# Gated mix of linear attention and a GEGLU block on one core: the handover from the first stage to the units, with a pool for the first stage's last results and a new order

## The chip, the cores and the metric

The kernel runs on one core of one Trainium2 chip. The metric is the device time in microseconds of one execution; lower is better. Three runs of the kernel before took 2373.40, 2373.74 and 2373.41 us, median 2373.41.

## The reference

All arrays are float32. `x` is 2048 tokens of 1024; 32 heads of 32; the inner width of the second block is 3584.

```
x = A_x
g = sigmoid((x * gate_w).sum(-1, keepdims=True))
q, k, v = split of x @ wqkv into heads
pq, pk  = q @ w_phi, k @ w_phi                       (per head)
phi(t)  = concat(softmax(t), softmax(-t))
kv = sum over s of phi(pk)^T v ;  z = sum over s of phi(pk)
a = ((phi(pq) @ kv) / (phi(pq) . z + 1e-6)) @ wo
b = (gelu(x @ w_gate) * (x @ w_up)) @ w_down
out = g * a + (1 - g) * b
```

## The kernel before, in words

Every float32 operand of a matmul is split into a high and a low half (ScalarE copies the high half, `high` L421 or `split` L43; VectorE subtracts for the low half, `low` L424 or L44), and three matmuls of the four products are made (`PASSES`). So a product of 128 x 1024 by 1024 x 512 is 24 matmuls of 128x512, and one over four blocks of 128 is 12.

The kernel has three parts.

*The first stage* (to L412; pools kw and kp, PSUM pools pd and pg) makes the keys and values for all tokens, their features, and sums kv and z over the tokens. Its last pieces are the tail of this study: `finish_kv` (L242) adds up kv in `kv_t` with `kv_l` and transposes it into `kv_c` (L254), which GpSimd's queue writes to the scratch tensor `kz` (L257); `finish_z` (L264) copies z into `zb` (L272), written to `kz` at L412. Both `kv_c` and `zb` are tiles of the pool kp. VectorE also makes `g_at` there, sixteen copies of 32x16 out of the gates `g_a` (L405 to L407); it is read only much later, by `attention` (L892). The first stage already makes some products of the second block: `first_g`, `first_u` (both halves of column block 0, on banks of pd), whose weights are in `first_w`.

*The handover* (L631 to L688, on all four engines written in the order in which the code stands, for VectorE, ScalarE, TensorE and SyncE). `gs` and `us` (L111, by `project`) are the gate and up products of column block 1, 2 x 24 matmuls each, on the four banks of pg. `gate_up` (L647) turns a gate product and an up product into a block of hidden values: gelu on ScalarE (L650), the product on VectorE (L651), and `spill` on GpSimd's queue into the scratch tensor `lm` (L139). The result `h` is a tile with three buffers (`hidden`, L476). At the same time `x_sums` (L485, VectorE, L488 to L491) makes four sums and differences of blocks of x out of a `raw` tile, for each of four `kc`; `highs` and `lows` make the halves of the four operands `xs` (tiles s1 to s4) from them. The raw tiles of kc 0 to 2 lie in the pool mid, the fourth in fp. `fp`, like `xa`, takes the place of kp, and a tile waits for everything that still uses the place where it lies. `start(weights(0, ...))` and `drain` let the generator that makes the first unit's weights take its steps (`wgu` for x, `tyz` for y and z, `v`).

*The units* (L764 on): 62 units of seven products of 12 matmuls, a Strassen-like scheme that makes four blocks out of seven products, on PSUM pools `pl` (a twice, p, c) and `pe` (c11, b, misc twice). `pe` lies where pg lay. The order of VectorE, ScalarE and SyncE in them comes from a planner: each generator yields (earliest slot, latest slot, VectorE's cost, ScalarE's cost), and `run_slot` lets those step for which there is room in a slot of 2.65. `background` runs the attention and the second half's sums in the slots' spare time, beginning with a first attention job in slot 13. `begin(t)` (L700) is one matmul that opens a bank for accumulation; before, all three `seeds` (c11, b, c) are begun right after the first product of the first unit (L783 to L785). After the units comes a last part (L1138 and so on) that multiplies by `wo` and `w_down`.

Of the kernel before, what the change touches and what calls it, by code (L numbers as in the profile page):

```python
# [8 lines left out]
F32 = mybir.dt.float32  # L9
# [7 lines left out]
P = 128  # L17
# [14 lines left out]
def tile_gated_mix(ctx: ExitStack, tc: tile.TileContext, x, xT, wkT, wqT, wv, w_phi, wo,  # L32
# [104 lines left out]
    def spill(h, dst, j, m):  # L137

        nc.gpsimd.dma_start(dst[m // 4][j, m % 2, :, m // 2 % 2, :], h)  # L139
# [9 lines left out]

    PE, DVE, ACT, SP = (getattr(mybir.EngineType, n) for n in ("PE", "DVE", "Activation", "SP"))  # L150
    with tc.tile_pool(name="kw", bufs=1) as kw, tc.tile_pool(name="kp", bufs=1) as kp, \
            tc.manual_schedule(engines={PE, DVE}):
        ones = kp.tile([P, P], F32, name="ones")
        nc.vector.memset(ones, 1.0)
        ones_r = kp.tile([P, P], F32R, name="ones_r")
# [86 lines left out]
        def finish_kv(hh, pkv):  # L242

            t = kp.tile([P, 4, 2, 2, 64], F32, tag="e", name="kv_t", bufs=2)
            for n, p in enumerate(pkv):
                nc.scalar.activation(t[:, n], p[:, :, 0], AF.Copy)
                nc.vector.tensor_tensor(t[:, n], p[:, :, 1], t[:, n], OP.add)
            low_rows = kp.tile([P, 4, 2, 2, 64], F32, tag="e", name="kv_l", bufs=2)
            nc.scalar.activation(low_rows[:64], t[64:], AF.Copy)
            nc.vector.tensor_tensor(t[:64], t[:64], low_rows[:64], OP.add)  # L250
            kv_c = kp.tile([P, 4, 2, 2, 32], F32, name="kv_c")
            for h in range(2):
                q = slice(32 * h, 32 * h + 32)
                nc.vector.transpose(kv_c[q].rearrange("p a b c d -> p (a b c) d"),  # L254
                                    t[q].rearrange("p a b c d -> p (a b c) d")[:, :, q])
            for s in range(2):
                nc.gpsimd.dma_start(kz[0][64 * s:64 * s + 64, 4 * hh:4 * hh + 4], kv_c[:64, :, :, s])  # L257
# [144 lines left out]
        nc.scalar.activation(g_a, logit, AF.Sigmoid)  # L402
        nc.vector.tensor_scalar(g_b, g_a, -1.0, 1.0, OP.mult, OP.add)
        nc.vector.tensor_scalar(g_n, g_a, 1.0, -1.0, OP.mult, OP.add)
        for h in range(4):  # L405
            for q in range(4):
                nc.vector.tensor_copy(g_at[32 * h:32 * h + 32, :, q], g_a[32 * q:32 * q + 32, :])  # L407
# [15 lines left out]
    def low(dst, src, dst_h):  # L423
        nc.vector.tensor_tensor(dst, src, dst_h.bitcast(F32), OP.subtract)  # L424
# [13 lines left out]
    with tc.tile_pool(name="xa", bufs=1) as xa, tc.tile_pool(name="fp", bufs=1) as fp, \  # L438
            tc.manual_schedule(engines={PE, DVE, ACT, SP}):
        xs = [(xa if k < 2 else fp).tile([P, 2, KC // 2, BLK], F32R, name=f"s{k + 1}") for k in range(4)]  # L440

# [27 lines left out]

        def hold(*parts):
            held.append(True)
            return len(held) - 1, stage(*parts, pool=fp if len(held) % 4 == 0 else None)

        def hidden():  # L476
            return fp.tile([P, BLK], F32, tag="h", name="h", bufs=3)


        def x_load(half, kc, r1, r2):  # L480
# [25 lines left out]
        def second_half(t, staging):  # L506
# [6 lines left out]

            while not free[0]:
                yield now[0] + 1, NEVER, 0.0
            raw = fp.tile([P, 2, 2 * BLK], F32, tag="pts", name="raw", bufs=1)
            staging = [*staging, raw[:, 0], raw[:, 1]]

            def load(n):
# [112 lines left out]
        raws.append(fp.tile([P, 2, 2 * BLK], F32, tag="pts", name="raw", bufs=1))  # L632
        for kc, r in enumerate(raws):
            if kc == 3:
                staged_up = stage((0, 1024, w_up[1]))
# [8 lines left out]
            for k, kc in which:  # L644
                low(xs[k][:, 1, kc, :], sums[kc][k], xs[k][:, 0, kc, :])

        def gate_up(g, u, m, js=range(2)):  # L647
            for j in js:
                h = hidden()
                nc.scalar.activation(h, g[j], AF.Gelu_apprx_tanh)  # L650
                nc.vector.tensor_tensor(h, u[j], h, OP.mult)  # L651
                spill(h, left_mlp[0], j, m)

        gs = [project(second_w, j) for j in range(2)]

# [18 lines left out]
        drain(-5)  # L674
        gate_up(gs, us, 1, [0])
        drain(-4)
        highs((2, 1), (3, 1))
        lows((2, 1), (3, 1))
        drain(-3)
        gate_up(gs, us, 1, [1])  # L680
        drain(-1)
        highs((2, 2), (3, 2), (2, 3), (3, 3))

        def late_lows():

            for at, which in ((1, [(2, 2), (3, 2)]), (4, [(2, 3)]), (6, [(3, 3)])):
                yield at, at, 0.7 * len(which)
                lows(*which)  # L688

# [74 lines left out]
        def unit(n, half, kind, m, before):  # L764
# [6 lines left out]
            for k in range(7):  # L771
                moved = True
                if k == 0 and before:
                    nc.scalar.activation(c, b, AF.Copy)
                elif k == 1:
                    nc.scalar.activation(c11, a, AF.Copy)
# [24 lines left out]
                kind_of[0] = kind, k  # L801
                run_slot(7 * n + k, 0.7 if fill else 0.0, 0.6 * moved + 1.2 * fill)
# [37 lines left out]
        def attention(jobs, between):  # L840
# [4 lines left out]
            while more:  # L845
# [54 lines left out]
                pts = fp.tile([P, 2, 2, BLK], F32R, tag="pts", name="pts", bufs=1)  # L900
# [279 lines left out]
```

## Time and profile before

| what | value |
| --- | --- |
| runs | 2373.40, 2373.74, 2373.41 us |
| profiled execution | 2372.92 us, of which the span is 2371.2 |
| TensorE busy in the span | 2358.3 us (99%) |
| VectorE busy | 1798.8 us (76%) |
| ScalarE busy | 1059.2 us (45%) |
| granted TensorE clock | 1.00 |
| the handover in the span | about 431 to 475 us |
| the units | about 461 to 1682 us |

In the views, PE is TensorE, PEld its weight load, DVE VectorE, ACT ScalarE, POOL GpSimd, SP SyncE; a q behind a name means the engine's queue, which issues and waits. A row of the timeline has the start, the length of the group of equal instructions in microseconds, the engine, the line, the operation, the tile written and those read, the shape and the count; in brackets stands how long the engine was idle before it and what released it. A view of waits has the waiting instruction, what it waited for, and then the total, the number of times and the longest.

### The profile page before, as it was taken

How to read it: one execution, taken by the hardware profiler on the slowest of the kernel's cores; microseconds unless marked ns; L12 is line 12 of the kernel's file. 1: busy time of each engine (PE TensorE's matmuls, PEld its weight loads, DVE VectorE, ACT ScalarE, POOL GpSimd, SP SyncE). 2: the span in 40 equal slices, each digit the busy share in tenths (PEclk: the TensorE clock that was granted, in tenths of full speed). 3: DMA queues.
4: the chain of work that ended last, by engine and by line, in shares of the span. 5: the costliest groups of instructions: out<-in, count | busy, mean ns of one | idle time of the engine just before them, and what ended most of it. 6: DMA issues, size and time to landing. Idle time of an engine off the chain costs nothing.

```text
span 2371.2 us, 28231 instructions
## 1 busy us (share of the span) xinstructions
PE 2358.3 (99%) x10625; PEld 1955.7 (82%) x10625; DVE 1798.8 (76%) x2321; ACT 1059.2 (45%) x1384; POOL 159.2 (7%) x297
## 2 busy tenths in 40 slices
PE   9999999999999999999999999999999999999999
PEld 8888888788888788888888888888888888888887
DVE  7887878878888787777778877888674868867873
ACT  4324332446455545455565656565533222323221
POOL 0000000011111011110000000000000000000000
PEclk9999999999999999999999999999999999999999
DMA  5112233554444366673444434434684767977874
GB/s 179 46 45 89 83 125 107 171 184 160 171 165 172 135 211 208 209 278 131 132 150 149 143 134 148 143 134 148 245 293 168 270 226 247 340 267 274 290 264 137
DMA packets 152617, 425.10 MB, mean 179 GB/s; under 512 B 21408, under 2 KB 21408, under 8 KB 152480
## 3 DMA queue, kind: packets, MB, share of 16 engines
q1 hardware_dynamic: 123840, 329.30, 41.3%
q0 software_dynamic: 27600, 93.87, 10.2%
q8 instruction: 83, 1.36, 0.2%
q14 instruction: 54, 0.44, 0.1%
q10 hardware_dynamic: 1040, 0.13, 0.0%
HBM read 328.34 MB, written 94.90 MB: 178 GB/s over the span
## 4 chain that ended last, share of the span: by engine, by line
PE 77%; DVE 2%; ACT 1%; issue 0%; DVEq 0%
PE po L1138 29%; PE a L743 20%; PE c L743 13%; PE b L743 7%; PE p L743 7%; PE misc L920 1%; ACT x L874 0%; DVE tyz L424 0%; DVE st L879 0%; ACT L874 0%; DVE x L882 0%; DVE x L869 0%; DVE h L720 0%; ACT h L924 0%; DVE wgu L424 0%
## 5 line engine op out<-in xcount | busy, mean ns | idle before, releaser
L206 PE MATMUL pd<-wkv,x 128*128 128x512 f32 x1536 | 359.8, 391 | 0.0
L206 PEld LDWEIGHTS pd<-wkv,x 128*128 128x128 f32 x1536 | 284.7, 188 | 57.2 <-DVE x L44 0.3
L1138 PE MATMUL po<-tw,wgu 128*128 128x512 f32 x1344 | 309.8, 389 | 0.0
L1138 PEld LDWEIGHTS po<-tw,wgu 128*128 128x128 f32 x1344 | 252.3, 188 | 52.4
L421 ACT ACTIVATE wgu<-stage 128x1024 fp32r<-128x1024 f32 x147 | 155.3, 1056 | 239.6 <-DVE stage L1028 161.4
L424 DVE TENSOR_TENSOR wgu<-stage,wgu 128x1024 fp32r<-128x1024 f32 x147 | 179.1, 1218 | 71.5 <-ACT wgu L421 70.6
L743 PE MATMUL a<-s,tyz 128*128 128x512 f32 x744 | 180.5, 390 | 2.1 <-DVE tyz L424 1.4
L743 PE MATMUL b<-s,tyz 128*128 128x512 f32 x744 | 179.0, 389 | 1.2 <-ACT b L778 1.2
L743 PE MATMUL a<-x,wgu 128*128 128x512 f32 x744 | 179.4, 390 | 0.7 <-DVE wgu L424 0.7
L743 PE MATMUL p<-s,tyz 128*128 128x512 f32 x744 | 179.1, 389 | 0.0
L743 PE MATMUL c<-x,tyz 128*128 128x512 f32 x744 | 178.8, 389 | 0.0
L743 PE MATMUL c<-x,wgu 128*128 128x512 f32 x744 | 178.7, 389 | 0.0
L743 PE MATMUL a<-s,v 128*128 128x512 f32 x744 | 178.7, 389 | 0.0
L421 ACT ACTIVATE tyz<-stage 128x1024 fp32r<-128x1024 f32 x126 | 132.7, 1053 | 91.0 <-DVE stage L569 37.7
L424 DVE TENSOR_TENSOR tyz<-stage,tyz 128x1024 fp32r<-128x1024 f32 x126 | 153.2, 1216 | 21.5 <-ACT tyz L421 21.2
L743 PEld LDWEIGHTS a<-s,tyz 128*128 128x128 f32 x744 | 139.1, 188 | 33.7 <-DVE tyz L424 3.6
L743 PEld LDWEIGHTS b<-s,tyz 128*128 128x128 f32 x744 | 139.5, 188 | 31.0 <-ACT b L778 2.0
L743 PEld LDWEIGHTS a<-x,wgu 128*128 128x128 f32 x744 | 139.0, 188 | 31.0 <-DVE wgu L424 1.1
L743 PEld LDWEIGHTS p<-s,tyz 128*128 128x128 f32 x744 | 139.4, 188 | 29.7 <-ACT x L756 0.6
L743 PEld LDWEIGHTS c<-x,tyz 128*128 128x128 f32 x744 | 139.6, 188 | 29.1
L743 PEld LDWEIGHTS a<-s,v 128*128 128x128 f32 x744 | 139.6, 188 | 29.0
L743 PEld LDWEIGHTS c<-x,wgu 128*128 128x128 f32 x744 | 139.6, 188 | 29.0
(189 smaller groups left out, 3530.7 us busy)
## 6 DMA issues: line engine op xcount, KB each, us to landing
stage<-lm SPq DMA_DIRECT2D x98, 512.0 KB, 4.7
sr<-in_w_down SPq DMA_DIRECT2D x84, 512.0 KB, 4.7
sl<-lm SPq DMA_DIRECT2D x70, 512.0 KB, 4.7
lm<-h POOLq DMA_DIRECT2D x112, 256.0 KB, 2.7
stage<-in_w_gate SPq DMA_DIRECT2D x43, 512.0 KB, 4.2
stage<-in_w_up SPq DMA_DIRECT2D x43, 512.0 KB, 4.1
stage<-la SPq DMA_DIRECT2D x28, 512.0 KB, 5.1
tg<-stage POOLq DMA_DIRECT2D x26, 512.0 KB, 3.0
```

Of the source, the lines that this page charges most:

```text
L206: nc.tensor.matmul(ps[m], xb[b, kc // 4][:, a, kc % 4, t * P:(t + 1) * P], w[:, e, m * 512:(m + 1) * 512], start=kc == 0 and i == 0, stop= ...
L421: nc.scalar.activation(dst, src, AF.Copy)
L424: nc.vector.tensor_tensor(dst, src, dst_h.bitcast(F32), OP.subtract)
L743: nc.tensor.matmul(dst, w[:, h, 4 * part + kc, :], xq[:, e, kc, :], start=first and kc == 0 and i == 0, stop=kc == 3 and i == 2, skip_grou ...
L920: nc.tensor.matmul(po[p], kbs[:, p].rearrange("p a b -> p (a b)"), pts[:, q, p, :], start=q == 0, stop=q == 1)
L1138: nc.tensor.matmul(ps[c], lefts[s][:, a, m, c * P:(c + 1) * P], made[k][:, e, m], start=d == 0 and m == 0 and n == 0, stop=d == n_duo - 1 ...
```

## The change

Five edits in the handover:

1. `zb` and `kv_c` go into a pool `kl` of their own. Of the second pool set, a part goes into a new pool `fa`, opened before fp: s3 and s4, the fourth raw tile and `pts` (which share a tag), the fourth staging tile, and h. fp keeps the rest (v, kz, kb, kbs, mm, st).
2. The 16 copies of `g_at` leave the first stage and are made by `background` in the units, four at a time from slot 9 on, planned with 0.8 each. `background` takes no other step before.
3. `gate_up` is cut into `gelu` and `multiply`, and the handover is written in another order: the up weights' low half right behind their high half, the gelus ahead of the high halves that stood in front of them, and the low halves of s2 of kc 2 and 3 later, in `late_lows`.
4. The drains of the first unit's weights stand at other places of this order.
5. `begin` is called for one seed each in the products k = 0, 3 and 6 of the first unit.

```
-            tc.manual_schedule(engines={PE, DVE}):
+            tc.tile_pool(name="kl", bufs=1) as kl, tc.manual_schedule(engines={PE, DVE}):
-        zb = kp.tile([P, NG, 2, 32], F32, name="zb")
+        zb = kl.tile([P, NG, 2, 32], F32, name="zb")
-            kv_c = kp.tile([P, 4, 2, 2, 32], F32, name="kv_c")
+            kv_c = kl.tile([P, 4, 2, 2, 32], F32, name="kv_c")
...
-        for h in range(4):
-            for q in range(4):
-                nc.vector.tensor_copy(g_at[32 * h:32 * h + 32, :, q], g_a[32 * q:32 * q + 32, :])
...
-        xs = [(xa if k < 2 else fp).tile(...) for k in range(4)]
+        xs = [(xa if k < 2 else fa).tile(...) for k in range(4)]
...
-        def gate_up(g, u, m, js=range(2)):
-            for j in js:
-                h = hidden()
-                nc.scalar.activation(h, g[j], AF.Gelu_apprx_tanh)
-                nc.vector.tensor_tensor(h, u[j], h, OP.mult)
-                spill(h, left_mlp[0], j, m)
+        def gelu(g):
+            h = hidden()
+            nc.scalar.activation(h, g, AF.Gelu_apprx_tanh)
+            return h
+
+        def multiply(h, u, j, m):
+            nc.vector.tensor_tensor(h, u, h, OP.mult)
+            spill(h, left_mlp[0], j, m)
...
         high(flat(up_w)[0], staged_up)
-        gate_up(first_g, first_u, 0)
         low(flat(up_w)[1], staged_up, flat(up_w)[0])
+        us = [project(up_w, j) for j in range(2)]
+        highs((2, 0), (3, 0))
+        for j in range(2):
+            multiply(gelu(first_g[j]), first_u[j], j, 0)
         lows((1, 0))
-        highs((2, 0), (3, 0))
         add(3)
-        us = [project(up_w, j) for j in range(2)]
+        hs = [gelu(gs[0])]
         start(weights(0, *units[0]))
         now[0] = -20
-        lows((2, 0), (3, 0), (1, 1), (1, 2), (1, 3))
-        drain(-5)
-        gate_up(gs, us, 1, [0])
+        lows((2, 0), (3, 0))
         drain(-4)
+        hs.append(gelu(gs[1]))
+        drain(-3)
         highs((2, 1), (3, 1))
+        lows((1, 1))
+        multiply(hs[0], us[0], 0, 1)
+        drain(-1)
         lows((2, 1), (3, 1))
-        drain(-3)
-        gate_up(gs, us, 1, [1])
-        drain(-1)
+        multiply(hs[1], us[1], 1, 1)
...
-                    if n == 0:
-                        for t in seeds:
-                            begin(t)
...
+                if n == 0 and k % 3 == 0:
+                    begin(seeds[k // 3])
...
-            yield 0, NEVER, 0.0
+            for q in range(4):
+                yield 9, NEVER, 0.8
+                for h in range(4):
+                    nc.vector.tensor_copy(g_at[32 * h:32 * h + 32, :, q], g_a[32 * q:32 * q + 32, :])
             rest = 0
+            yield now[0], NEVER, 0.0
```

The changed kernel's lines are numbered a little otherwise: L424 becomes L421, L421 becomes L418, L743 becomes L746, L702 becomes L705, L488 to L491 become L486 to L489, and L650 becomes L647 (L651 stays).

The order of the instructions is shown at three places. On TensorE at the first unit, before (a, p, c11, b and c are banks; rows of L702 are the flags):

```order
L743 MATMUL a_3617<-x10_2481,wgu_3578 128x512 x12
L702 MATMUL c11_3614<-x10_2481 128x512
L702 MATMUL b_3615<-x10_2481 128x512
L702 MATMUL c_3619<-x10_2481 128x512
L743 MATMUL p_3618<-s1_3409,tyz_3591 128x512 x12
L743 MATMUL a_3617<-s2_3410,tyz_3635 128x512 x12
L743 MATMUL c11_3614<-x11_2676,wgu_3578 128x512 x12
```

The same place in the changed kernel:

```order
L746 MATMUL a_3606<-x10_2484,wgu_3568 128x512 x12
L705 MATMUL c11_3603<-x10_2484 128x512
L746 MATMUL p_3607<-s1_3400,tyz_3575 128x512 x12
L746 MATMUL a_3606<-s2_3401,tyz_3624 128x512 x12
L705 MATMUL b_3604<-x10_2484 128x512
L746 MATMUL c11_3603<-x11_2679,wgu_3568 128x512 x12
L746 MATMUL b_3604<-s3_3402,tyz_3575 128x512 x12
L705 MATMUL c_3608<-x10_2484 128x512
```

The flags of b and c stand directly ahead of, or some products ahead of, the first product on their banks; that of c11 stands where it stood.

On VectorE at the end of the first stage, before (g_b and g_n are the gates' other forms, the first wgu row is the low half of `second_w`):

```order
L404 TENSOR_SCALAR g_n<-g_a 128x16
L407 COPY g_at<-g_a 32x16 x16
L44 TENSOR_TENSOR wgu<-stage,wgu 128x1024
L247 TENSOR_TENSOR kv_t<-pg,kv_t 128x256 x4
L490 TENSOR_TENSOR raw<-raw 128x512
L491 TENSOR_TENSOR raw<-raw 128x512
L250 TENSOR_TENSOR kv_t<-kv_t,kv_l 64x1024
L424 TENSOR_TENSOR s_3409<-raw,s_3409 128x512
L254 STREAM_TRANSPOSE kv_c<-kv_t 32x512 x2
```

The same place in the changed kernel:

```order
L404 TENSOR_SCALAR g_n<-g_a 128x16
L44 TENSOR_TENSOR wgu<-stage,wgu 128x1024
L488 TENSOR_TENSOR raw<-raw 128x512
L489 TENSOR_TENSOR raw<-raw 128x512
L247 TENSOR_TENSOR kv_t<-pg,kv_t 128x256 x4
L421 TENSOR_TENSOR s_3400<-raw,s_3400 128x512
L486 TENSOR_TENSOR raw<-raw 128x512
L250 TENSOR_TENSOR kv_t<-kv_t,kv_l 64x1024
L487 TENSOR_TENSOR raw<-raw 128x512
L254 STREAM_TRANSPOSE kv_c<-kv_t 32x512 x2
```

The copies are gone, and two more of the sums stand ahead of the transposes.

On VectorE from the fourth raw block's low halves (s3, kept by number) to the last product of `us` (h<-pg), before:

```order
L424 TENSOR_TENSOR s_3412<-raw,s_3412 128x512
L424 TENSOR_TENSOR s_3410<-raw,s_3410 128x512 x3
L651 TENSOR_TENSOR h<-pg,h 128x512
L424 TENSOR_TENSOR wgu<-stage,wgu 128x1024
L424 TENSOR_TENSOR s_3411<-raw,s_3411 128x512
L424 TENSOR_TENSOR s_3412<-raw,s_3412 128x512
L568 TENSOR_TENSOR stage<-stage 128x512
L569 TENSOR_TENSOR stage<-stage 128x512
L651 TENSOR_TENSOR h<-pg,h 128x512
```

The same place in the changed kernel:

```order
L421 TENSOR_TENSOR s_3403<-raw,s_3403 128x512
L421 TENSOR_TENSOR wgu<-stage,wgu 128x1024
L566 TENSOR_TENSOR stage<-stage 128x512
L567 TENSOR_TENSOR stage<-stage 128x512
L421 TENSOR_TENSOR s_3401<-raw,s_3401 128x512
L651 TENSOR_TENSOR h<-pg,h 128x512
L421 TENSOR_TENSOR tyz<-stage,tyz 128x1024
L570 TENSOR_TENSOR stage<-stage 128x512
L571 TENSOR_TENSOR stage<-stage 128x512
L421 TENSOR_TENSOR s_3402<-raw,s_3402 128x512
L421 TENSOR_TENSOR s_3403<-raw,s_3403 128x512
L651 TENSOR_TENSOR h<-pg,h 128x512
```

The low half of the first unit's weights (wgu) comes right behind the low halves of the first kc, and the last product now has the low half of a tyz and two further sums ahead of it. After the handover each engine has its old order, but for the copies of g_at behind a tyz in the second unit.

More of the change, by code (lines that the diff above doesn't have):

```diff
@@ L436, in right_block @@
         return src[4 * d * P:4 * (d + 1) * P, c * BLK:(c + 1) * BLK].rearrange("(m r p) n -> r p m n", r=2, p=P)[r]
-    with tc.tile_pool(name="xa", bufs=1) as xa, tc.tile_pool(name="fp", bufs=1) as fp, \
+    with tc.tile_pool(name="xa", bufs=1) as xa, tc.tile_pool(name="fa", bufs=1) as fa, \
+            tc.tile_pool(name="fp", bufs=1) as fp, \
             tc.manual_schedule(engines={PE, DVE, ACT, SP}):
-        xs = [(xa if k < 2 else fp).tile([P, 2, KC // 2, BLK], F32R, name=f"s{k + 1}") for k in range(4)]
+        xs = [(xa if k < 2 else fa).tile([P, 2, KC // 2, BLK], F32R, name=f"s{k + 1}") for k in range(4)]
         SLOT, NEVER = 2.65, 10 ** 9
@@ L473, in hold @@
             held.append(True)
-            return len(held) - 1, stage(*parts, pool=fp if len(held) % 4 == 0 else None)
+            return len(held) - 1, stage(*parts, pool=fa if len(held) % 4 == 0 else None)
         def hidden():
-            return fp.tile([P, BLK], F32, tag="h", name="h", bufs=3)
+            return fa.tile([P, BLK], F32, tag="h", name="h", bufs=3)
         def x_load(half, kc, r1, r2):
@@ L515, in second_half @@
                 yield now[0] + 1, NEVER, 0.0
-            raw = fp.tile([P, 2, 2 * BLK], F32, tag="pts", name="raw", bufs=1)
+            raw = fa.tile([P, 2, 2 * BLK], F32, tag="pts", name="raw", bufs=1)
             staging = [*staging, raw[:, 0], raw[:, 1]]
@@ L631, in tile_gated_mix @@
         raws = [mid.tile([P, 2, 2 * BLK], F32, tag="tyz", name="raw", bufs=3) for _ in range(3)]
-        raws.append(fp.tile([P, 2, 2 * BLK], F32, tag="pts", name="raw", bufs=1))
+        raws.append(fa.tile([P, 2, 2 * BLK], F32, tag="pts", name="raw", bufs=1))
         for kc, r in enumerate(raws):
@@ L664, in tile_gated_mix @@
         high(flat(up_w)[0], staged_up)
[L665 removed]
         low(flat(up_w)[1], staged_up, flat(up_w)[0])
+        us = [project(up_w, j) for j in range(2)]
+        highs((2, 0), (3, 0))
+        for j in range(2):
+            multiply(gelu(first_g[j]), first_u[j], j, 0)
         lows((1, 0))
[L668 removed]
         add(3)
[L670 removed]
+        hs = [gelu(gs[0])]
         start(weights(0, *units[0]))
         now[0] = -20
[L673 to L675 removed]
+        lows((2, 0), (3, 0))
         drain(-4)
+        hs.append(gelu(gs[1]))
+        drain(-3)
         highs((2, 1), (3, 1))
+        lows((1, 1))
+        multiply(hs[0], us[0], 0, 1)
+        drain(-1)
         lows((2, 1), (3, 1))
[L679 to L681 removed]
+        multiply(hs[1], us[1], 1, 1)
         highs((2, 2), (3, 2), (2, 3), (3, 3))
         def late_lows():
[L686 removed]
+            for at, which in ((0, [(1, 2), (1, 3)]), (2, [(2, 2), (3, 2)]), (4, [(2, 3)]), (6, [(3, 3)])):
                 yield at, at, 0.7 * len(which)
@@ L899, in attention @@
                 yield now[0], NEVER, 1.3
-                pts = fp.tile([P, 2, 2, BLK], F32R, tag="pts", name="pts", bufs=1)
+                pts = fa.tile([P, 2, 2, BLK], F32R, tag="pts", name="pts", bufs=1)
                 nc.vector.transpose(wide[1], wide[0])
```

## Prediction

> **What bounds the kernel now.** I read the page first, then the waits of TensorE, then the stretch in which those waits lie as a timeline of TensorE, then the same stretch for the engines that it waits for. The page:
>
> ```profile
> span 2371.2 us, 28231 instructions
> PE 2358.3 (99%) x10625; PEld 1955.7 (82%) x10625; DVE 1798.8 (76%) x2321; ACT 1059.2 (45%) x1384; POOL 159.2 (7%) x297
> ```
>
> TensorE is busy for 99% of the span, and the change takes no matmul away. All that can be won is TensorE's idle time, 2371.2 - 2358.3 = 12.9 us. Who ends it is in the waits of TensorE (total, times, longest):
>
> ```profile
> PE pd L161 <- DVE ones L154: 2.3, 1, 2.3
> PE c L702 <- DVE h L651: 2.3, 1, 2.3
> PE a L743 <- DVE tyz L424: 1.4, 3, 0.5
> ...
> PE a L743 <- ACT c L776: 0.7, 2, 0.4
> PE a L743 <- DVE wgu L424: 0.7, 1, 0.7
> ```
>
> The first row is the start of the kernel. The second, the last and part of the others lie in one place, the handover from the first stage to the units. TensorE there (start, length of the group, matmuls, idle before and its releaser), and behind it one later row of the chain that ended last, for the pace of twelve matmuls:
>
> ```profile
> 438.86 22.13 PE L111 MATMUL pg<-x,wgu 128*128 128x512 f32 x96
> 460.82 0.61 PE L743 MATMUL a<-x,wgu 128*128 128x512 f32 x2
> 462.12 2.58 PE L743 MATMUL a<-x,wgu 128*128 128x512 f32 x10 [0.68 <-DVE wgu L424]
> 467.00 0.50 PE L702 MATMUL c<-x 128*128 128x512 f32 x1 [2.30 <-DVE h L651]
> ...
> 467.80 2.91 PE L743 MATMUL p<-s,tyz 128*128 128x512 f32 x12
> 471.10 3.36 PE L743 MATMUL a<-s,tyz 128*128 128x512 f32 x12 [0.38 <-ACT c L776]
> 474.30 2.88 PE L743 MATMUL c<-x,wgu 128*128 128x512 f32 x12
> ```
>
> ```profile
> 477.18 2.72 PE b L743 x12
> ```
>
> From 438.86 to 474.30 are 35.44 us. In it stand 96 + 12 + 3 + 12 + 12 = 135 matmuls of 128x512, which at 2.72 / 12 = 0.2267 us take 30.60 us. **The handover loses 4.84 us**, and from 474.30 on the pace is full. This is the ceiling of the change, as long as nothing after the handover moves.
>
> Why TensorE waits there is in the timeline of all engines:
>
> ```profile
> 431.71 2.97 DVE L407 COPY g_at<-g_a 32x16 f32<-32x16 f32 x16
> ...
> 438.92 2.21 ACT L272 ACTIVATE zb<-pg 32x128 f32<-32x128 f32 x8
> ...
> 440.25 1.41 DVE L254 STREAM_TRANSPOSE kv_c<-kv_t 32x512 f32<-32x512 f32 x2
> ...
> 445.89 0.88 SPq L483 DMA_DIRECT2D raw<-in_xT  x2
> ...
> 453.85 0.69 DVE L488 TENSOR_TENSOR raw<-raw 128x512 f32<-128x512 f32 x1 [3.06 <-DMA raw<-in_xT]
> ...
> 456.64 3.69 DVE L424 TENSOR_TENSOR s<-raw,s 128x512 fp32r<-128x512 f32 x6
> ...
> 460.85 1.21 DVE L424 TENSOR_TENSOR wgu<-stage,wgu 128x1024 fp32r<-128x1024 f32 x1
> ...
> 464.68 1.06 ACT L421 ACTIVATE tyz<-stage 128x1024 fp32r<-128x1024 f32 x1 [5.55 <-issue]
> 465.64 0.58 ACT L650 ACTIVATE h<-pg 128x512 f32<-128x512 f32 x1
> 466.25 0.69 DVE L651 TENSOR_TENSOR h<-pg,h 128x512 f32<-128x512 f32 x1 [1.66 <-ACT h L650]
> ```
>
> It is one chain. The fourth raw block of x is asked for only at 445.89, so VectorE stands until 453.85. Then it is late with the low half of the first unit's weights (460.85 to 462.06, TensorE wanted it at 460.82). ScalarE is late with the last gelu, which stands behind the high half of tyz (464.68), and so the last product of the first stage ends at 466.94. On that product the first flag waits, at 467.00. What holds the load of x is in the waits of SyncE's queue:
>
> ```profile
> SPq L483 <- DMA kz<-kv_c: 26.3, 1, 26.3
> SPq L483 <- DMA kz<-zb: 0.8, 1, 0.8
> ```
>
> The raw block lies where zb and kv_c lay, so it waits until both are written out.
>
> **The change part by part.** *A pool of their own (kl), and fa.* The load of the fourth raw block no longer waits for kz<-kv_c and kz<-zb, only for the last reader of its place, the transposes. *The 16 copies of g_at leave the first stage*: VectorE is free of them at 431.71 instead of 434.68. From there to the end of the transposes it worked 441.66 - 434.71 = 6.95 us. In the new order two more sums stand in between; four sums take 456.64 - 453.85 = 2.79, so two take 1.40. The transposes end at 431.7 + 6.95 + 1.40 = 440.1, and the load goes out at about 440.2, 5.7 us sooner. With the old 453.85 - 445.89 = 7.96 to the first use it is there at 448.2.
>
> *The new order on VectorE.* From 448.2: four sums 2.79; three low halves of s at 3.69 / 6 = 0.615, 1.85; wgu 1.21; two sums 1.40; one s 0.62; a product 0.69; tyz 1.21; two sums 1.40; two s 1.23. That is 12.4 us, to 460.6. The low half of wgu is done at 454.0, 6.6 us before TensorE's first unit asks for it (438.86 + 96 x 0.2267 = 460.6): the 0.68 goes. The last product then needs the last of the 96 matmuls, done at 460.99, and ends at about 461.7. TensorE comes to the first flag at 460.6 + 2.72 = 463.3. **The 2.30 goes, with 1.6 us to spare.** The third operand's halves now come while TensorE is still at the unit's first product; before, the copy of a into c11 stood behind its high half on ScalarE (0.38 idle) and its low half came in the middle of the group of 471.10, which lasts 3.36 instead of 2.88. Both go.
>
> *The new wait that this order makes.* The fourth h takes the first h's buffer (three of them), which is free when that h is written out. Before, that gelu stood at 465.64 and nobody saw it. Now it stands on ScalarE ahead of the high half of tyz, and behind it waits VectorE's tyz, so the chain above. The rows for its price, from the same timeline:
>
> ```profile
> 445.85 1.28 ACT L650 ACT_TABLE_LOAD   x1 [0.40 <-DMA kz<-zb]
> ...
> 447.77 1.29 DVE L651 TENSOR_TENSOR h<-pd,h 128x512 f32<-128x512 f32 x2 [2.61 <-ACT h L650]
> 448.11 1.16 ACT L421 ACTIVATE s<-raw 128x512 fp32r<-128x512 f32 x2
> ...
> 448.75 1.14 POOL L139 DMA_DIRECT2D lm<-h  x2 [4.84 <-DVE h L651]
> ```
>
> And the times from issue to landing: in the DMA view of 445 to 462 us the median of these writes, in the tile view of lm least, median and most of all four writes of the handover, and in the tile view of stage the same for the loads of 410 to 432 us:
>
> ```profile
> lm<-h POOLq DMA_DIRECT2D x3, 256.0 KB, 9.2
> ```
>
> ```profile
> DMA to landing us min/median/max: 2.3/5.8/9.8
> ```
>
> ```profile
> DMA to landing us min/median/max: 5.5/8.7/11.8
> ```
>
> ScalarE ends zb at 441.13; then come one high half of s (0.58), wgu (1.06), two of s (1.16), the table load (1.28) and a gelu (0.58): 445.8. With 0.69 for the product and 0.29 to the write (448.75 - 448.46) it goes out at 446.8. The bounds of its landing are 2.3 and 11.8; I take 9.2, the row of the same write in the same crowd of loads, so 456.0. Then gelu 0.58 and tyz high 1.06 end at 457.7, where the chain would have had it at 456.7; the last product ends at 462.3 and **1.1 us are left**. At 2.3 the wait is not there, at 11.8 TensorE stands 1.5 us.
>
> What stands in the way of these writes is in the first of two rows of the view by windows (its DMA share is 0.98, at 392 GB/s; the columns before are the busy time of PE, PEld, DVE, ACT and POOL, and PEclk):
>
> ```profile
> 452.00:458.00 6.00, 6.00 (x28) 4.97 (x27) 4.05 (x7) 2.60 (x5) 0.00 (x0) 1.00 0.98 392
> 475.00:495.00 20.00, 20.00 (x90) 16.57 (x89) 11.13 (x15) 8.72 (x13) 4.15 (x8) 1.00 0.62 222
> ```
>
> The Trainium skill, "DMA: Bandwidth & Descriptors", section "Queues, rings and completion order", has each DMA engine take turns between its queues, a packet from each; by that the write would not stand behind SyncE's six loads, and my estimate from this page is that it lands some 5 us after its issue, with no wait at all. The 9.2 us of the row speak against so even a share, so I keep the row; the sum is the same by both, only the spare time differs.
>
> *Flags one by one.* Three single matmuls are spread over the first unit instead of standing together. Only the first waited; the other two keep their 0.23 us each. Worth 0, cost 0: the banks of b and c were released by the same products or earlier.
>
> *The g_at copies in the units* cost 2.97 us of VectorE at about 478 us, behind the low half of a tyz and ahead of the low half of the third unit's wgu. In the second window row VectorE is busy for 11.13 of 20.00 us, so 5.9 us stay free with them, and wgu is asked for by TensorE a whole unit (19.0 us) after the one before. Cost 0; without this cover at most 2.97.
>
> **The sum.** The profiled execution is 2372.92 us (2371.2 of span and 1.72 around it), 0.49 below the median of the runs, 2373.41. 2372.92 - 4.84 = 2368.1; from the median, which I give, **2368.6**. The measurement of this kernel can tell about 0.2%, 4.75 us, from no change: the ceiling is just on that line.
>
> **The rivals.** *A: the write of the first h lands late.* Beyond 9.2 + 1.1 = 10.3 us each microsecond of its landing is one of TensorE's. For it: all loads start together again, and the write is issued last of them. Against: they start 5.7 us sooner and the write only 2 us sooner, so more of them is through. At 11.8: 2370.1; at 13: 2371.3.
>
> *B: it is given back in the units.* The copies, the shifted writes, or the order of the first unit's weights meet a unit that has no slack, and up to 2.97 us return: 2371.6. Against it stands the free time of the window row, and that from the second unit on each engine has its old order but for the copies.
>
> *C: the wait grows beyond the old one, and the kernel is slower.* Same place as A, from the point where the write takes 10.3 + 4.84 = 15.1 us: the first flag then waits longer than all the handover lost before. At 18 us it is 2376.3. No row of this window is near it (most 11.8). Here a rule of the skill, "TensorE: Matmul & The Clock Gate", section "Why this matters for your kernels", would add to it: idle gaps over some 3 us let TensorE's clock fall to half, which the granted clock of 1.00 around the 2.30 us gap can neither show nor exclude.
>
> *D: nothing changes*, because the load of x is held by another wait for its place that the last one hid: 2373.4. Against it, the order has no DMA ahead of that load but those that landed by 430 us.
>
> **How the numbers follow.** Forecast 0.75, A 0.13, B 0.05, C 0.04, D 0.03. The four times shown before spread over 2372.92 to 2373.74, so half that, 0.4, and 0.2 for the pace stand around the forecast: 2368.0 to 2369.2. A and B widen it to 2371.2, which leaves out the far end of A, C, D and part of B, under 0.15. The line of 0.2% is 2368.66, 0.06 above the forecast: of its 0.75 I count 0.44 as faster and 0.31 as the same. Same also are A, B and D with 0.21; C is 0.04, and 0.00 more for anything else: faster 0.44, same 0.52, slower 0.04.
>
> **What would show it.** In the changed profile: the load of the fourth raw block at about 440.2; the low half of wgu near 454; the last product of the first stage at 461.5 to 462.5; TensorE's matmuls from 438.86 on without idle time, the first flag at 463.3, the c11 group at 469.5 instead of 474.30; the waits of TensorE without the L702 row; the g_at copies near 478 with nobody waiting. I am wrong if the flag still waits (then ScalarE's last gelu has a DMA as its releaser: A or C), or if TensorE gains new waits after 475 (B).

## The result, and the profile after

The changed kernel takes 2368.52 us (median of 12 executions, 2368.30 to 2369.23), the kernel before beside it on the same chip 2373.72 us (12 executions, 2373.32 to 2374.83). The ratio is 0.9978, with a 95% interval of 0.9969 to 0.9987. The slowest of the 12 lies 4.09 us below the fastest of before, and the interval leaves out 1, but it reaches across the prediction's line of 0.2% (0.998), right beside which the forecast lay. The profiled execution took 2368.36 us.

The page of the changed kernel, span and busy times:

```profile
span 2366.6 us, 28230 instructions
...
PE 2357.4 (100%) x10625; PEld 1957.4 (83%) x10625; DVE 1798.7 (76%) x2321; ACT 1059.2 (45%) x1384; POOL 159.2 (7%) x297
```

The span is 4.6 us shorter, and no engine has noticeably less to do. What went is idle time, and the waits of TensorE say which (total, times, longest):

```profile
PE pd L161 <- DVE ones L154: 2.3, 1, 2.3
PE a L746 <- DVE tyz L421: 1.4, 3, 0.5
PE b L746 <- ACT b L781: 1.2, 2, 0.6
PE a L746 <- ACT c L779: 0.3, 1, 0.3
```

The wait for the last product (2.3) and that for the low half of wgu (0.7) are gone, and the waits for c are 0.3 where they were 0.7. Nothing new stands in the list. The handover itself, in the timeline of the changed kernel, rows of all engines in order of time:

```profile
438.89 1.41 DVE L254 STREAM_TRANSPOSE kv_c<-kv_t 32x512 f32<-32x512 f32 x2
...
439.19 21.92 PE L111 MATMUL pg<-x,wgu 128*128 128x512 f32 x96
...
440.45 0.88 SPq L481 DMA_DIRECT2D raw<-in_xT  x2
...
446.74 1.14 POOL L139 DMA_DIRECT2D lm<-h  x2 [4.17 <-DVE h L651]
...
447.76 0.69 DVE L486 TENSOR_TENSOR raw<-raw 128x512 f32<-128x512 f32 x1
...
452.36 1.22 DVE L421 TENSOR_TENSOR wgu<-stage,wgu 128x1024 fp32r<-128x1024 f32 x1
452.86 0.60 ACT L647 ACTIVATE h<-pg 128x512 f32<-128x512 f32 x1 [0.85 <-DMA lm<-h]
...
454.98 1.06 ACT L418 ACTIVATE tyz<-stage 128x1024 fp32r<-128x1024 f32 x1 [1.53 <-DVE stage L567]
...
460.95 2.88 PE L746 MATMUL a<-x,wgu 128*128 128x512 f32 x12
461.15 0.69 DVE L651 TENSOR_TENSOR h<-pg,h 128x512 f32<-128x512 f32 x1 [1.08 <-PE pg L111]
...
463.67 0.39 PE L705 MATMUL c<-x 128*128 128x512 f32 x1
...
469.56 2.88 PE L746 MATMUL c<-x,wgu 128*128 128x512 f32 x12
...
478.15 1.84 DVE L825 COPY g_at<-g_a 32x16 f32<-32x16 f32 x10
```

From the 96 matmuls (439.19) to the c11 group (469.56) are 30.37 us for 134 matmuls, which is 134 x 0.2267: the handover loses nothing. (One flag fewer than before stands ahead of that group.) The start lies 0.33 us later than in the profiled execution of before, and 4.84 - 0.33 = 4.5 is the 4.6 by which the span fell, within 0.1. The load of the fourth raw block goes out at 440.45, right behind the transposes that make kv_c (438.89 to 440.30). For them, and for no write into kz, SyncE's queue now waits ahead of it:

```profile
SPq L481 <- DVE kv_c L254: 21.6, 1, 21.6
```

The first sum of that block (447.76) waits for no DMA. The last product waits 1.08 us for TensorE, where before it waited for ScalarE, and it ends at 461.84, 1.83 us ahead of the flag.

### The profile page after: what moved, and what is told of

It reads as the page before. It is cut to its first block, busy times and chain, and to the rows that moved or that the text cites. A ratio compares the mean times of both kernels' runs of the same rounds, so it can differ in the third digit from the quotient of the medians.

```text
span 2366.6 us, 28230 instructions
## 1 busy us (share of the span) xinstructions
PE 2357.4 (100%) x10625; PEld 1957.4 (83%) x10625; DVE 1798.7 (76%) x2321; ACT 1059.2 (45%) x1384; POOL 159.2 (7%) x297
## 4 chain that ended last, share of the span: by engine, by line
PE 97%; DVE 2%; ACT 1%; issue 0%; DVEq 0%
PE po L1144 29%; PE a L746 21%; PE pd L206 15%; PE c L746 13%; PE b L746 7%; PE p L746 7%; PE pg L239 1%; PE misc L926 1%; PE pd L111 1%; PE pg L111 1%; PE pd L144 1%; ACT x L880 0%; PE pg L196 0%; PE pd L196 0%; DVE tyz L421 0%
## 5 line engine op out<-in xcount | busy, mean ns | idle before, releaser
L418 ACT ACTIVATE wgu<-stage 128x1024 fp32r<-128x1024 f32 x147 | 155.3, 1056 | 239.7 <-DVE stage L1034 160.6
L421 DVE TENSOR_TENSOR wgu<-stage,wgu 128x1024 fp32r<-128x1024 f32 x147 | 179.1, 1218 | 70.6 <-ACT wgu L418 69.8
L746 PE MATMUL a<-s,tyz 128*128 128x512 f32 x744 | 180.0, 390 | 1.7 <-DVE tyz L421 1.4
L746 PE MATMUL b<-s,tyz 128*128 128x512 f32 x744 | 179.1, 389 | 1.2 <-ACT b L781 1.2
L746 PE MATMUL a<-x,wgu 128*128 128x512 f32 x744 | 179.1, 390 | 0.0
L746 PE MATMUL p<-s,tyz 128*128 128x512 f32 x744 | 179.0, 389 | 0.0
L746 PE MATMUL c<-x,tyz 128*128 128x512 f32 x744 | 178.8, 389 | 0.0
L746 PE MATMUL a<-s,v 128*128 128x512 f32 x744 | 178.7, 389 | 0.0
L746 PE MATMUL c<-x,wgu 128*128 128x512 f32 x744 | 178.7, 389 | 0.0
L418 ACT ACTIVATE tyz<-stage 128x1024 fp32r<-128x1024 f32 x126 | 132.7, 1053 | 86.5 <-DVE stage L567 39.0
L421 DVE TENSOR_TENSOR tyz<-stage,tyz 128x1024 fp32r<-128x1024 f32 x126 | 153.2, 1216 | 21.6 <-ACT tyz L418 21.2
L746 PEld LDWEIGHTS a<-s,tyz 128*128 128x128 f32 x744 | 139.3, 188 | 32.6 <-DVE tyz L421 3.1
L746 PEld LDWEIGHTS b<-s,tyz 128*128 128x128 f32 x744 | 139.5, 188 | 31.0 <-ACT b L781 2.0
L746 PEld LDWEIGHTS p<-s,tyz 128*128 128x128 f32 x744 | 139.5, 188 | 29.5 <-ACT x L759 0.6
L746 PEld LDWEIGHTS a<-x,wgu 128*128 128x128 f32 x744 | 139.1, 188 | 30.0 <-DVE x L714 0.7
L746 PEld LDWEIGHTS c<-x,tyz 128*128 128x128 f32 x744 | 139.6, 188 | 29.1
L746 PEld LDWEIGHTS a<-s,v 128*128 128x128 f32 x744 | 139.7, 188 | 29.0
L746 PEld LDWEIGHTS c<-x,wgu 128*128 128x128 f32 x744 | 139.7, 188 | 29.0
```

The costliest lines, as they stand in the source:

```text
L418: nc.scalar.activation(dst, src, AF.Copy)
L746: nc.tensor.matmul(dst, w[:, h, 4 * part + kc, :], xq[:, e, kc, :], start=first and kc == 0 and i == 0, stop=kc == 3 and i == 2, skip_grou ...
```

## The experiments

Theory: the load that zb and kv_c held back is the root, and pools, copies and order each take a part of the same delay. Rivals: that one edit alone is all of it; that the copies of g_at are paid in full wherever VectorE is late; that the flags count. In all runs the figure read from the trace is TensorE's time from the start of the 96 matmuls to the start of the c11 group, less 0.2267 us for each matmul in it (135 with all three flags ahead, 30.60 us; 134 else, 30.37).

**e1: the pools alone.** The kernel before with

```
-        zb = kp.tile([P, NG, 2, 32], F32, name="zb")
+        zb = kl.tile([P, NG, 2, 32], F32, name="zb")
...
-        raws.append(fp.tile([P, 2, 2 * BLK], F32, tag="pts", name="raw", bufs=1))
+        raws.append(fa.tile([P, 2, 2 * BLK], F32, tag="pts", name="raw", bufs=1))
```

and in the same way kv_c, s3, s4, the fourth staging tile, pts and h.

> The kernel before with the two new pools alone (zb and kv_c out of the place that the fourth raw block, the h tiles and the last sums take); the copies, the order and the flags stay as before. Theory (the load of the fourth raw block, held back by the writes of kz, is the root; the order carries what is left): the load goes out at about 440.5 us and the products of the handover lose 0.8 to 1.6 us in place of 4.84, so some 3.4 us of the 5 us come with the pools alone: 2369.9 to 2370.8 us. Rival 1 (the order and the moved copies are the gain, the load is only along for the ride): at most 1 us comes, 2372.7 us or more. Rival 2 (the pools are all of it): the products lose less than 0.3 us, 2368.3 to 2368.9 us.

Measured: 2369.88 us against 2373.72 (ratio 0.9984, 0.9975 to 0.9993). The timeline of SyncE and of TensorE:

```profile
442.65 0.88 SPq L484 DMA_DIRECT2D raw<-in_xT  x2
```

```profile
439.58 21.92 PE L111 MATMUL pg<-x,wgu 128*128 128x512 f32 x96
461.34 2.88 PE L744 MATMUL a<-x,wgu 128*128 128x512 f32 x12
464.33 0.50 PE L703 MATMUL c<-x 128*128 128x512 f32 x1
464.67 0.40 PE L703 MATMUL b<-x 128*128 128x512 f32 x1
...
468.43 3.34 PE L744 MATMUL a<-s,tyz 128*128 128x512 f32 x12 [0.40 <-ACT c L777]
471.61 2.88 PE L744 MATMUL c<-x,wgu 128*128 128x512 f32 x12
```

32.03 - 30.60 = 1.43 us are lost, so 3.41 of the 4.84 come with the pools: the theory's size, and neither rival. The load goes out later than the 440.5 expected, since the copies still stand ahead of the transposes. The flag is 0.27 late (461.34 + 2.72 = 464.06), and the copy of a into c11 still stands behind the high half of tyz on ScalarE.

**e2: everything but the pools.** The changed kernel with the first diff turned round.

> The changed kernel with zb, kv_c, the fourth raw block, the h tiles and the last sums back in the pools of before; copies, order and flags as changed. Theory (the load is the root): the load of the fourth raw block waits again for the writes of kz, goes out at about 446 us, and the high halves that the new order puts ahead of the products stand still for it: TensorE loses 1.4 to 6 us in the handover, 2370.0 to 2375 us. Rival (the order carries the gain by itself): less than 0.5 us is lost, 2368.3 to 2369.0 us.

Measured: 2369.91 us (0.9984, 0.9975 to 0.9993). SyncE and TensorE:

```profile
444.83 0.88 SPq L480 DMA_DIRECT2D raw<-in_xT  x2
```

```profile
439.49 21.92 PE L111 MATMUL pg<-x,wgu 128*128 128x512 f32 x96
461.25 2.88 PE L745 MATMUL a<-x,wgu 128*128 128x512 f32 x12
465.11 0.47 PE L704 MATMUL c<-x 128*128 128x512 f32 x1 [0.98 <-DVE h L650]
...
471.12 2.88 PE L745 MATMUL c<-x,wgu 128*128 128x512 f32 x12
```

1.26 us are lost, just under the theory's range. It is more than the rival (order alone carries it) allows, but it is far from making the pools indispensable: with the load still held by kz, copies and order recover 3.6 of the 4.84. So the gain is not a sum of parts; the parts overlap. That called for the single ones and the other pair.

**e3: the copies of g_at back in the first stage**, the rest as changed (the loop of 16 copies behind `g_n`, the four steps of `background` taken out).

> The changed kernel with the 16 copies of g_at (2.97 us) back where they stood before, ahead of the handover on VectorE; everything else as changed. VectorE's last product of the handover waited 1.08 us for TensorE, and TensorE came to the flag 1.83 us after that product, so VectorE has 2.9 us to spare there. Theory (only what exceeds this spare time costs): 0 to 1.1 us are lost, most likely 0.1, 2368.4 to 2369.6 us. Rival (the copies were a part of the gain in full): 2.97 us are lost, 2371.5 us.

Measured: 2368.46 us (0.9978, 0.9969 to 0.9986), as the changed kernel. In the trace the 96 matmuls start at 439.74 and the c11 group at 470.12, 30.38 us: nothing is lost. The load goes out at 442.69, the last product ends at 463.79, and the flag stands at 464.22: 0.43 us to spare. The copies eat the spare time and cost nothing. The rival of 2.97 us falls.

**e4: all three flags behind the first product**, as before (edit 5 undone).

> The changed kernel with all three flags set right after the first product, as before, in place of one by one. Theory (the flags one by one are worth nothing, since the last product of the handover ends 1.83 us ahead of the first flag, and all banks are free by then): no difference over 0.2 us, 2368.3 to 2368.8 us, the three flags stand one behind the other at about 463.7 us. Rival (one of the other two banks is still read then): TensorE waits ahead of the second product for 0.5 to 2 us, 2369.0 to 2370.5 us.

Measured: 2368.42 us (0.9978, 0.9969 to 0.9987). The flags stand at 463.77, 464.00 and 464.22 without a wait between; 439.29 to 469.89 is 30.60 us, nothing lost. The flags one by one are worth nothing here.

**e5: the moved copies alone**, on the kernel before.

> The kernel before with the 16 copies of g_at alone moved into the units; pools, order and flags as before. Theory (the start of the raw load is what counts, and the copies stood ahead of the transposes of kv_c whose write into kz holds it): the load still waits for kz, but goes out 1 to 2 us sooner than before, counted from the start of the 96 products, and the handover loses 2.6 to 3.8 us in place of 4.84: 2371.5 to 2372.7 us. Rival (VectorE's work by itself sets the end, so all 2.97 us come): 1.9 us are lost, 2370.8 us. Rival (the copies lay in idle time anyway): nothing comes, 2373.7 us.

Measured: 2371.49 us against 2373.55 (0.9992, 0.9983 to 1.0001, an interval that takes in no change). TensorE:

```profile
439.18 21.92 PE L111 MATMUL pg<-x,wgu 128*128 128x512 f32 x96
460.94 2.88 PE L740 MATMUL a<-x,wgu 128*128 128x512 f32 x12
465.76 0.50 PE L699 MATMUL c<-x 128*128 128x512 f32 x1 [1.94 <-DVE h L648]
...
466.56 4.49 PE L740 MATMUL p<-s,tyz 128*128 128x512 f32 x12
470.89 2.89 PE L740 MATMUL a<-s,tyz 128*128 128x512 f32 x12
473.62 2.88 PE L740 MATMUL c<-x,wgu 128*128 128x512 f32 x12
```

The load goes out at 444.88, 5.70 us behind the start of the 96, where it was 445.89 - 438.86 = 7.03 before: 1.33 sooner, as the theory has it. 3.84 us are lost in this execution. Of these, 1.61 have nothing to do with a wait: the twelve matmuls of p last 4.49 instead of 2.88 us. That is the clock (last section). Without it, 2.23 are lost, less than the 2.6 to 3.8 of the theory and nearer to the 1.9 of the first rival. The times speak for the theory: the median of the nine executions at full clock, 2371.48 us, is 3.0 above that of e7 in the same call, which loses nothing (below), and the rivals have 2370.8 and 2373.7. So 2.2 to 3.0 us are lost here, and the theory's size is borne out only in part.

**e6: the new order alone**: neither pools nor moved copies.

> The changed kernel with both pools undone and the copies of g_at back in the first stage: what is left is the new order of the handover (and the flags, which run e4 showed to be worth nothing). Theory (order and copies together recovered 3.6 us with the load still held; each of them gets a part): the load goes out as late as before, VectorE waits for it, and the handover loses 2.5 to 4 us, 2371.4 to 2372.9 us. Rival (the new order alone is what recovered the 3.6 us): 1.3 us are lost, 2369.9 us. Rival (the order is harmful while the load is held, since the high halves stand ahead of the products): more than 4.84 us are lost, 2374 us or more.

Measured: 2372.87 us against 2373.55 (0.9997, 0.9989 to 1.0006). The load goes out at 446.53, VectorE waits 2.46 us for it, and TensorE waits 2.88 us for the last product. 4.64 us are lost in the profiled execution, above the theory's range; 1.26 of them are again a slow p group (4.14 us), and the 3.38 without it lie inside; some 0.2 more come from the flag, which is slow too (0.56 us to the next matmul, 0.31 in e2). The rival "order alone recovers 3.6" falls, and 2372.87 us is not the 2374 or more of the rival that the order does harm.

**e7: pools and moved copies, the order of before.**

> The kernel before with the pools and the moved copies, and the order and the flags of before: the new order is left out. Theory (what has to come is 4.84 us; pools alone gave 3.4 of them, and the copies take another 2.97 us off VectorE's queue ahead of the last product): nothing is lost, 2368.3 to 2368.9 us, and the new order is not needed. Rival (the new order is a part that nothing else replaces): 1.0 to 1.5 us are lost, 2369.5 to 2370.0 us.

Measured: 2368.46 us (0.9979, 0.997 to 0.9988), as the changed kernel. TensorE and VectorE:

```profile
439.29 21.92 PE L111 MATMUL pg<-x,wgu 128*128 128x512 f32 x96
461.05 2.88 PE L741 MATMUL a<-x,wgu 128*128 128x512 f32 x12
463.77 0.39 PE L700 MATMUL c<-x 128*128 128x512 f32 x1
...
469.92 2.88 PE L741 MATMUL c<-x,wgu 128*128 128x512 f32 x12
```

```profile
461.90 0.69 DVE L649 TENSOR_TENSOR h<-pg,h 128x512 f32<-128x512 f32 x1 [1.66 <-ACT h L648]
```

The last product still stands behind ScalarE's high half of tyz, as before. But it starts 4.35 us sooner (466.25 there, 461.90 here), and it ends 1.18 us ahead of the flag. 0.03 us are lost. The new order isn't needed when pools and copies are there.

What the handover loses in each profiled execution, with the time against that of before in the same call:

| what is changed | lost, us | of it a slow p group | time less before's, us |
| --- | --- | --- | --- |
| nothing | 4.84 | 0 | 0 |
| order (e6) | 4.64 | 1.26 | -0.68 |
| copies (e5) | 3.84 | 1.61 | -2.06 |
| pools (e1) | 1.43 | 0 | -3.84 |
| copies, order (e2) | 1.26 | 0 | -3.81 |
| pools, order (e3) | 0.01 | 0 | -5.26 |
| pools, copies (e7) | 0.03 | 0 | -5.09 |
| pools, copies, order; flags together (e4) | 0.00 | 0 | -5.30 |
| the change | 0.00 | 0 | -5.20 |

The pools are the largest single part, and together with either of the two others they bring all. Without the slow p groups the three single edits bring 3.41, 2.61 and 1.46 us, together more than the 4.84 that there are: they overlap.

**e9, e10, e11: how much time is to spare, and what it costs beyond.** The changed kernel with N = 6, 14 and 22 additions put on VectorE ahead of `multiply(hs[0], us[0], 0, 1)`:

```
+        pad = fp.tile([P, 192], F32, name="pad")
+        nc.vector.memset(pad, 0.0)
+        for _ in range(N):
+            nc.vector.tensor_tensor(pad, pad, pad, OP.add)
```

> The changed kernel with 6 additions of a scratch tile (128x192) and its memset put on VectorE right ahead of the third product of the handover. By the rows of 128x512 (0.69 us) and 128x256 (0.41 us) one takes about 0.37 us with its gap, together with the memset 2.5 us. VectorE's spare time there is 0.20 + 1.08 us of waits for TensorE and the 1.83 us by which the last product is ahead of the flag, 3.1 us. Theory (only what exceeds the spare time costs): nothing is lost, 2368.2 to 2368.8 us, the flag comes right behind the last product. Rival (the chain through VectorE is already at the limit): 2.5 us, 2371 us.

> The same with 14 additions, 5.4 us with the memset: 2.3 us beyond the spare time. Theory: TensorE stands 2.3 us ahead of the flag, and with the slow restart 2.4 us are lost: 2370.9 us. With the half clock for about 3 us that two of the earlier runs showed behind a pause of 1.9 and 2.9 us, 1.3 to 1.6 us more in those executions that have it: 2372.3 us, and a wider spread. Rival (a granted clock that falls only behind pauses over 3 us): no half clock here, 2370.9 us in all executions.

> The same with 22 additions, 8.4 us with the memset: 5.3 us beyond the spare time. Theory: TensorE stands 5.3 us ahead of the flag, 5.4 us are lost, and behind so long a pause the half clock comes in every execution (some 1.5 us more): 2375.4 us, slower than the kernel before. Rival (the pause alone counts, the clock stays): 2373.9 us, as before.

Measured: 2368.46, 2372.35 and 2377.07 us against 2373.23 (ratios 0.998 with 0.9971 to 0.9989, 0.9995 with 0.9986 to 1.0004, 1.0015 with 1.0007 to 1.0024). With 6, the additions and the memset take 2.33 + 0.22 us, and the flag stands at 463.67, as without them. With 14, the additions on VectorE, the flag on TensorE, and then the view by windows, where the number behind the five busy times is the granted clock:

```profile
455.82 5.47 DVE L684 TENSOR_TENSOR pad<-pad 128x192 f32<-128x192 f32 x14
```

```profile
466.30 0.47 PE L709 MATMUL c<-x 128*128 128x512 f32 x1 [2.50 <-DVE h L651]
466.61 4.51 PE L750 MATMUL p<-s,tyz 128*128 128x512 f32 x12
```

```profile
466.00:467.00 1.00, 0.70 (x3) 0.64 (x4) 1.00 (x3) 0.84 (x2) 0.54 (x1) 1.00 1.02 418
467.00:468.00 1.00, 1.00 (x5) 0.82 (x4) 1.00 (x2) 1.00 (x2) 0.00 (x0) 0.68 0.52 197
468.00:469.00 1.00, 1.00 (x4) 0.72 (x4) 1.00 (x2) 0.35 (x1) 0.00 (x0) 0.50 0.25 90
469.00:470.00 1.00, 1.00 (x4) 0.81 (x3) 1.00 (x3) 0.00 (x0) 0.00 (x0) 0.50 0.62 66
```

5.47 + 0.22 - 3.1 = 2.6 us beyond the spare time, and the flag is 466.30 - 463.64 = 2.66 us late. With 22 it is 8.62 + 0.22 - 3.1 = 5.7, and the flag, at 469.45, is 5.8 us late. So the spare time of 3.1 us is right to 0.1, and each microsecond beyond it is one of TensorE's. Then comes the half clock: with 14, the clock is down for some 3 us and costs another 1.6 in the profiled execution (4.51 us for p instead of 2.88). The mean clock is below 1 in 6 of the 11 executions (median 2372.79 us) and 1 in the other 5 (2371.46); with 22 it is below 1 in all 11. The 2377.07 us with 22 are 1.7 above what was expected (2375.4): the clock stays down for some 7 us in place of 3, and from the flag to the end of p that costs 2.6 us (5.66 in place of the 3.07 of e2) where 1.5 had been put.

**e8: a version that beats both.** The three waits for tyz that are left come from ScalarE in the units: in the first two of them (1147 and 1384 us) a table load and four exponentials stand ahead of the copies and of the high half of tyz. The changed kernel with

```
-                yield now[0] + 1, NEVER, 0.0, 2.4
+                yield now[0] + 1, NEVER, 0.0
+                while kind_of[0] == ("u", 6) and now[0] < 345:
+                    yield now[0] + 1, NEVER, 0.0
+                yield now[0], NEVER, 0.0, 2.4
```

`kind_of` holds the unit's kind and the product that is running (0 to 6), and 345 is a number of a slot.

> The changed kernel with one more rule in the units: the four exponentials of an attention step aren't begun in the last seventh of an up unit (before turn 345), because ScalarE's table load and exponentials (1.28 and 2.56 us) stand there ahead of the copies and of the high half tyz for which TensorE waits at about 1147 and 1384 us. Theory (those waits are 0.5 us each, with the slow restart 0.7): both go and nothing new comes, 1.4 us faster than the changed kernel, 2367.0 to 2367.5 us. Rival (the exponentials come to stand ahead of another copy): the waits only move to other places, 2368.2 to 2369 us.

Measured: 2366.86 us (7 executions, 2366.39 to 2367.08) against 2373.55 (0.9973, 0.9962 to 0.9984). Its range lies wholly below that of the changed kernel (2368.30 to 2369.23, another call) and of e7 in the same call (2367.92 to 2368.65); it is 6.69 us below before, where the change was 5.20, and a little below the 2367.0 to 2367.5 expected. The row of that wait among the waits of TensorE, and ScalarE where the first of the three was:

```profile
PE a L746 <- DVE tyz L421: 0.3, 1, 0.3
```

```profile
1139.50 1.05 ACT L418 ACTIVATE tyz<-stage 128x1024 fp32r<-128x1024 f32 x1
1140.56 1.28 ACT L883 ACT_TABLE_LOAD   x1
1141.86 2.57 ACT L883 ACTIVATE x<-x 64x512 f32<-64x512 f32 x4
1144.34 0.57 ACT L779 ACTIVATE c<-a 128x512 f32<-128x512 f32 x1
```

The high half of tyz now stands ahead of the table load, two of the three waits are gone, and the list has no new row.

## Why the prediction was right, point by point

- *The ceiling of 4.84 us in the handover, all of it won.* Right: 30.37 us for 134 matmuls.
- *The chain, with the held load as its root.* Right in its steps and times. Load at 440.45 (440.2 predicted), first sum at 447.76 (448.2), low half of wgu done at 453.58 (454.0), last product done at 461.84 (461.7, or 462.3 with the wait for the write), flag at 463.67 (463.3), c11 group at 469.56 (469.5). Run e1 shows that the pools alone bring 3.41 of the 4.84. But e2 recovers 3.58 with the load still held by kz, so setting the load free is the largest single part and not one without which nothing is won. What the prediction did not see is how much the change has to spare: it worked out all edits as one chain, and e3 and e7 show that without the moved copies, or without the new order, the handover is as full.
- *The new wait for the write of the first h.* The wait came, but its term was mis-sized: the write took 452.86 - 446.74 = 6.1 us, not 9.2. The gelu waited 0.85 us, and after it ScalarE waited 1.53 us for VectorE anyway, so it cost nothing. 1.83 us are to spare, not 1.1. The estimate of some 5 us from the Trainium skill, "DMA: Bandwidth & Descriptors", section "Queues, rings and completion order", was nearer to it than the row of before. The prediction's own argument against rival A, that more of the loads is through when this write goes out, fits the runs: the median of the first two of these writes is 9.5 us before and 8.2, 7.7 and 7.3 in e5, e6 and e2, where kz holds the load, and 4.9, 6.1, 5.6 and 6.3 in e1, e3, e7 and the changed kernel, where it goes out early. e1 differs from before in the pools alone.
- *Flags one by one: nothing.* Right, by e4. *Copies in the units: nothing.* Right: they run at 478.15, and TensorE has no wait from there to 784 us. That they could have stayed in the first stage too is e3.
- *Rivals.* A: the write landed well under the 10.3 us from which it would count. B: no wait appeared in the units; the remaining ones stand where they stood before, 4.5 us sooner. D: SyncE's waits have no row for kz any more. C's mechanism, a flag that waits longer than all the old waits together, is real but was not met here; e11 makes it by hand, with additions on VectorE in place of a late write, and at 5.6 us of wait the kernel is 3.84 us slower than before.
- *The size in the median.* 5.20 us against 4.84 worked out. A part of the rest may be the clock, for which the sum had no term: the profiled execution of before ran at full clock, but of the 89 executions of before timed beside the experiments 51 have a mean granted clock of 0.999, and their medians lie 0.24, 0.51 and 0.31 us above those of the others in the three calls. The changed kernel has no wait at the flag, and none of its 12 executions has that clock. Against the executions of before at full clock alone (medians 2373.53, 2373.10 and 2373.17), e3, e7 and e9, which lose nothing either, gain 5.07, 4.64 and 4.71 us, on both sides of 4.84. That the median came within 0.1 us of the forecast of 2368.6 is in part luck: the base of 2373.41, from three runs, lay 0.31 under the later 2373.72, and the gain came out 0.36 larger than worked out.

## What to carry to other kernels

When a load goes out late, look at what wrote out of the place that its tile takes: a tile of a closed stage that is still on its way to memory holds a load that shares nothing with it but the address. Before several edits are worked through as one chain, ask which of them would do alone; here the pools with either of two others made the whole difference, and the rest became spare time. And measure the spare time itself, by padding the engine that ends last: it told within 0.1 us from where a delay costs.

## What the runs showed of the hardware that was not expected

*Half the clock after a pause of two microseconds.* In the profiled executions with waits of 1.94 (e5), 2.88 (e6) and 2.50 us (e10) TensorE's granted clock fell to 0.50 for some 3 us around the end of the wait or up to 1.1 us behind it; with 5.63 us (e11) it was down from about 468 to 475. With the 2.30 us of before and the 0.98 of e2 it stayed at 1.00. So the length of the pause does not decide by itself: 1.94 us brought the fall, and 2.30 did not. Of the other executions only the mean clock is known. It is 0.999 in 2, 6, 6 and 11 of the 11 executions of e5, e6, e10 and e11, and in the first three each of these is slower than each with a mean of 1; in e2 it is 1 in all 11. The fall costs 1.5 to 1.6 us, in e11 2.6. What decides whether it comes, no run here shows. The Trainium skill, "TensorE: Matmul & The Clock Gate", section "Why this matters for your kernels", warns of gaps over some 3 us; here shorter ones were enough. Its section "What's actually happening" has the monitor's window run freely, which would fit a fall by chance; no run here tested the phase.

*A restart costs some 0.1 us.* After a pause, the second matmul starts 0.34 us behind the first (464.33 to 464.67 in e1) or 0.31 (465.11 to 465.42 in e2) instead of 0.23.

*Writes among loads.* The writes into kz, in the DMA view of 438 to 460 us of before and then of the changed kernel (size, median from issue to landing):

```profile
kz<-zb POOLq DMA_DIRECT2D x1, 256.0 KB, 2.4
kz<-kv_c POOLq DMA_DIRECT2D x2, 64.0 KB, 2.2
```

```profile
kz<-zb POOLq DMA_DIRECT2D x1, 256.0 KB, 7.8
kz<-kv_c POOLq DMA_DIRECT2D x2, 64.0 KB, 6.1
```

With the loads free to start together with them, the same writes took about three times as long. The pools alone make the difference: it is 7.9, 7.9 and 7.6 us for zb in e1, e3 and e7, and 2.4 in e2, e5 and e6, where the pools are those of before. SyncE's queue does not wait for these writes any more, so it cost nothing here; a kernel that reads them soon could see it.
